# The second feed-forward's first rows, loaded ahead of the last two experts' scatters, and their transposes spread out

## The chip, the core and the metric

The kernel runs on one core of a Trainium2 chip. The metric is the device time of one execution in microseconds (us). Five engines work side by side, each through its own queue in order: TensorE (PE; its weight loads are listed as PEld), VectorE (DVE), ScalarE (ACT), GpSimd (POOL) and SyncE (SP), which issues most of the transfers (DMA). Semaphores order work between engines.

## What is computed

Three stages, each feeding the next, on 1536 tokens of 512 features in float32:

```python
# 1 attention, 2 x 8 heads, 768 positions, 64 wide: sinks 0..3 and a window of 128
a = softmax(where(keep, q @ k.T / 8, -1e9)); x = (a @ v)                     # -> 1536 x 512
# 2 mixture of experts: each token goes to one of 8 experts, at most 384 tokens each
e = argmax(x @ w_gate); h = relu(x[tokens of e] @ w1[e]); y = gate * (h @ w2[e])
# 3 second feed-forward, weights stored as 64-bit floats
out = square(relu(y @ w_in)) @ w_out                                         # 512 -> 2048 -> 512
```

Tokens that an expert has no place for give zeros.

## The kernel before, in words

Products are made three times over: each float32 factor is split into a high part (a copy rounded to the format fp32r, on ScalarE) and a low part (the difference, on VectorE), and high x high, high x low and low x high are summed in PSUM. So each weight and each activation costs ScalarE a copy and VectorE a subtraction (`split`, L141; `pre_split`, L704; L938 and L939; `go`, L1045 and L1046).

**Experts.** The tokens of an expert are worked in blocks of 128 rows. `body(e, b, ...)` (L905) is block b of expert e: the first product in two halves (`g1`), relu, transposes of the hidden values (`tr`, tiles hT, hTh, hTl), the second product in four groups of six matmuls (`g2`), the gate (L981, tile ys) and a scatter of the 128 rows by GpSimd into the table yd in DRAM (L982). Block (e, 0) always runs; `more` (L988) holds blocks 1 and 2 in branches that are taken when the expert has that many tokens (L994). In yd the rows are packed by expert, each with its token's number in an extra column; empty places go out of bounds and aren't written. `pre(e, b)` (L896) transposes a block's gathered rows into xT.

The order of the work is written out by hand. `body` has five points at which it runs functions handed to it (`also`), and a plan that says after which group how many `splits` run. For expert 7 the splits are ticks (`Ticks`, L191): each tick stages one piece of the second feed-forward's weights (1 MB: `piece_load`, L158; L180 to L188) through four steps on ScalarE and VectorE, and the plan LAST (L24) puts three ticks into block (7, 0). A piece's load goes out on SP as soon as the raw buffers that it needs are freed by an earlier split or tick (`freed`, `pull`).

**Second feed-forward.** It takes yd in three chunks of 512 rows. `load_y(c, tags)` (L1027) issues three loads of 128 rows each on SP (`ld`, L1034, tiles xb), and gives back four functions; function t (`go`, L1036) transposes tile t on TensorE (L1040, four transposes into one PSUM bank, tile x2T), copies the tokens' numbers on POOL (L1042), splits the result into the two x2A tiles (L1045, L1046) and, the first of them, issues the fourth load. For chunk 0, load_y is called when expert 7 begins, ahead of block (7, 0). Its loads depend on the scatters into yd that stand ahead of them in the program, so on those of experts 0 to 6. Where they have to be read again, since rows below 512 belong to expert 7, a branch behind expert 7 does so (L1097 to L1102): it compares `head`, the rows ahead of expert 7 (L1068), with 512. The functions 0 to 2 are run at point 4 of block (7, 0), behind its last `g2` and ahead of its last tick and of the gate; function 3 at point 0 of block (7, 1) (L1088, L1092).

Behind expert 7 come `ticks.close()` (L1108), twelve writes that clear the output (L1116), and the steps `stage_a` and `stage_b` (L1121, L1177), one tick beside each of the first.

By the reference's inputs the experts get 290, 123, 98, 163, 117, 165, 92 and 488 tokens, the last cut to 384. So there are 14 blocks, expert 5 has two, expert 6 one and expert 7 three, and 956 rows stand ahead of expert 6.

Of the kernel before, what the change touches and what calls it, by code (L numbers as in the profile page):

```python
# [16 lines left out]
P = 128  # L17
# [15 lines left out]
def kernel(  # L33
# [15 lines left out]
    nc = tc.nc  # L49
    B, H, S, D = q.shape  # L50
    NTOK, DM = out.shape
    E = w_gate.shape[1]
# [33 lines left out]
    def ps(tag, name):  # L86
        banks[tag].append(banks[tag].pop(0))
        return psum.tile([P, 512], F32, tag=f"b{banks[tag][-1]}", name=name)
# [127 lines left out]
    yd = dram.tile([NTOK, DM + 1], F32, name="yd")  # L216
# [107 lines left out]
    if fast:  # L324
# [22 lines left out]
        for g in range(3 if stack else 1):  # L347
            x = own[g * HS : (g + 1) * HS]
# [352 lines left out]
    def gate_at(e, b):  # L701
        return gate[2 + b % 2 if b else e % 2]
# [7 lines left out]
    def pre_gate(e, b, sums):  # L710
        g_ = gate_at(e, b)
        nc.vector.tensor_scalar(g_, sums, 1e-9, None, op0=ALU.add)
        nc.vector.reciprocal(g_, g_)
# [90 lines left out]
    for u in range(len(units) + PL + 1):  # L804
# [4 lines left out]
        if u < len(units):  # L809
            n, c = units[u]  # L810
# [17 lines left out]
        m, c = divmod(u, HP)  # L828
# [13 lines left out]
        if u % 4 == 2:  # L842
            r0 = u // 4 * P
# [41 lines left out]
    def x_at(e, b):  # L885
        return xring[min(b, XB - 1), e % 2]

    def load_x(e, b):
        if e >= E or b >= nblk:
            return  # L890
        nc.gpsimd.indirect_dma_start(
            out=x_at(e, b), out_offset=None, in_=xd[:, :], in_offset=bass.IndirectOffsetOnAxis(ap=src[:, b, e : e + 1], axis=0),
            bounds_check=NTOK - 1, oob_is_err=False,
        )

    def pre(e, b):  # L896
        if e >= E or b >= nblk:
            return
        p_ = ps("bg", "xT")
        for c in range(KD):  # L900
            nc.tensor.transpose(p_[:, c * P : (c + 1) * P], x_at(e, b)[:, c * P : (c + 1) * P], ident)
        pre_split(e, b, p_)
        pre_gate(e, b, x_at(e, b)[:, DM:])

    def body(e, b, splits, plan, also):  # L905
        xh, xl = xT[e, b]
        wts = W[e]
        splits = list(splits)

        def sp(n):  # L910
            for _ in range(n):
                if splits:
                    splits.pop(0)()

        hs = mp.tile([P, F], F32, tag="hs", name="hs", bufs=1)
        hp = [None, None]

        def g1(half, ks):
            if ks[0] == 0:
                hp[half] = ps("s" if half or b else "iv", "h")  # L920
            for kk in ks:
                r = slice(half * 512, half * 512 + 512)
                for m, (a, bb) in enumerate(((xh, wts.h), (xh, wts.l), (xl, wts.h))):
                    nc.tensor.matmul(hp[half], a[:, kk, :], bb[kk][:, r], start=(kk == 0 and m == 0), stop=(kk == KD - 1 and m == 2))

        def relu(half):
            nc.scalar.activation(hs[:, half * 512 : half * 512 + 512], hp[half], AF.Relu)

        hT = [None, None]

        def tr(half):
            p_ = ps("pt", "hT")
            for c in range(4):
                o0 = half * 512 + c * P
                nc.tensor.transpose(p_[:, c * P : (c + 1) * P], hs[:, o0 : o0 + P], ident)
            h_ = mp.tile([P, 512], F32R, tag="hTh", name="hTh", bufs=2)
            l_ = mp.tile([P, 512], F32R, tag="hTl", name="hTl", bufs=2)
            nc.scalar.copy(h_, p_)  # L938
            nc.vector.tensor_sub(l_, p_, h_.bitcast(F32))  # L939
            hT[half] = (h_, l_)  # L940

        y = ps("ot", "y")

        def g2(fs):
            for f in fs:
                h_, l_ = (x[:, (f % 4) * P : (f % 4 + 1) * P] for x in hT[f // 4])
                wh, wl = wts.h[KD + f // 2], wts.l[KD + f // 2]
                r = slice((f % 2) * 512, (f % 2) * 512 + 512)
                for m, (a, bb) in enumerate(((h_, wh), (h_, wl), (l_, wh))):
                    nc.tensor.matmul(y, a, bb[:, r], start=(f == 0 and m == 0), stop=(f == NF - 1 and m == 2))  # L950

        def point(i):
            for f in also.get(i, ()):
                f()

        plan = iter(plan)
        g1(0, [0, 1, 2, 3])
        sp(next(plan))
        relu(0)
        g1(1, [0, 1])  # L960
        sp(next(plan))
        tr(0)
        g1(1, [2, 3])
        sp(next(plan))
        relu(1)
        point(0)
        g2([0, 1])
        sp(next(plan))
        tr(1)
        point(1)  # L970
        g2([2, 3])
        point(2)
        sp(next(plan))
        g2([4, 5])
        point(3)
        g2([6, 7])
        point(4)
        sp(next(plan))
        y_ = mp.tile([P, DM + 1], F32, tag="ys", name="ys", bufs=2)
        nc.gpsimd.tensor_copy(y_.bitcast(I32)[:, DM:], src[:, b, e : e + 1])  # L980
        nc.vector.tensor_scalar(y_[:, :DM], y, gate_at(e, b), None, op0=ALU.mult)  # L981
        nc.gpsimd.indirect_dma_start(  # L982
            out=yd[:, :], out_offset=bass.IndirectOffsetOnAxis(ap=dst[:, b, e : e + 1], axis=0), in_=y_, in_offset=None,
            bounds_check=NTOK - 1, oob_is_err=False,
        )
        sp(len(splits))

    def more(e, b, also=()):  # L988
# [27 lines left out]
    def split_at(g, i):  # L1016
        W[g].split(i, nc.gpsimd if i in SPOOL else None, nc.vector.tensor_copy if i in SDVE else None)
# [6 lines left out]
    last = (E - 1) % 2  # L1024
    yts = [xring[b, 1 - last] for b in range(XB)]

    def load_y(c, tags):  # L1027

        c0, w = chunks[c]

        def ld(t):
            if t < w // P:
                r0 = c0 + t * P
                nc.sync.dma_start(yts[t % len(yts)], yd[r0 : r0 + P, :])  # L1034

        def go(t):  # L1036
            yt = yts[t % len(yts)]
            p_ = ps(tags[t % 2], "x2T")
            for kk in range(KD):
                nc.tensor.transpose(p_[:, kk * P : (kk + 1) * P], yt[:, kk * P : (kk + 1) * P], ident)  # L1040
            n = c0 // P + t
            nc.gpsimd.tensor_copy(tok[:, n : n + 1], yt.bitcast(I32)[:, DM:])  # L1042
            pv = p_.rearrange("p (k n) -> p k n", k=KD)
            hv, lv = (x[:, :, t * P : (t + 1) * P] for x in x2T[c])
            nc.scalar.copy(hv, pv)  # L1045
            nc.vector.tensor_sub(lv, pv, hv.bitcast(F32))  # L1046
            ld(t + len(yts))

        for t in range(len(yts)):
            ld(t)  # L1050
        return [lambda t=t: go(t) for t in range(w // P)]
# [8 lines left out]
    if nblk:  # L1060

        off = const.tile([P, E], F32, name="off")
        nc.vector.memset(off[:, 0:1], 0.0)  # L1063
        for e in range(1, E):
            nc.vector.tensor_add(off[:, e : e + 1], off[:, e - 1 : e], cntf[:, e - 1 : e])
        cnt = const.tile([P, E + 2], I32, name="cnt")
        nc.vector.tensor_copy(cnt[:, :E], cntf)
        nc.vector.tensor_copy(cnt[:, E : E + 1], off[:, E - 1 :])  # L1068
        nc.vector.tensor_add(cnt[:, E + 1 :], off[:, E - 1 :], cntf[:, E - 1 :])
        dst = const.tile([P, nblk, E], I32, name="dst")  # L1070
        nc.vector.tensor_add(free, free, spot.unsqueeze(2).to_broadcast([P, nblk, E]))
        nc.vector.tensor_add(dst, free, off.unsqueeze(1).to_broadcast([P, nblk, E]))
    vals = {}
    its = []
    for e in range(E):
        g = e + 1
        if e > 0:
            W[g].alloc()
        for b in range(1, XB):
            load_x(e + 1, b)  # L1080
        if g < E:
            splits = [(lambda i=i, g=g: split_at(g, i)) for i in range(16)]
        else:
            splits = [ticks.tick] * (NPRE + 1)
            its = load_y(0, ("bg", "bg"))
        if nblk:
            also = {2: [lambda: pre(e, 1), lambda: pre(e + 1, 0), lambda: load_x(e + 2, 0)]}
            also[4] = its[:-1]  # L1088
            body(e, 0, splits, HEAVY if g < E else LAST, also)
            if nblk > 1:  # L1090
                vals[e] = nc.values_load(cnt[0:1, e : e + 1], min_val=0, max_val=cap)
            more(e, 1, its[-1:])  # L1092
        else:
            for f in splits + its:
                f()
    if nblk:
        head = nc.values_load(cnt[0:1, E : E + 1], min_val=0, max_val=NTOK)  # L1097
        total = nc.values_load(cnt[0:1, E + 1 :], min_val=0, max_val=NTOK)

        with tc.If(head < CH):  # L1100
            for f in load_y(0, ("pt", "ot")):
                f()  # L1102
# [16 lines left out]
    outp, gT, its, scattered = {}, {}, [], []  # L1119
# [178 lines left out]
```

## Time and profile before

| | |
|---|---|
| median of 3 runs | 599.48 us (598.98 to 600.80) |
| the profiled execution | 599.34 us |
| its span, first to last instruction | 597.6 us |
| PE, PEld busy | 571.6 us (96%), 456.2 us (76%) |
| DVE, ACT, POOL busy | 354.2, 296.7, 138.8 us |
| bytes moved | 82.09 MB, mean 137 GB/s |

Times are from the span's start. Attention fills the first 130 us or so, the experts follow up to about 322 us, then the second feed-forward up to the end. "Busy" counts an engine's instructions that run, not how near they are to the engine's peak; the idle time of an engine that nobody waits for costs nothing.

### The profile page before, as it was taken

What the parts mean: (1) busy time and instruction counts of PE and PEld (TensorE: products, weight loads), DVE (VectorE), ACT (ScalarE), POOL (GpSimd) and SP (SyncE); (2) the same over time, 40 slices, a digit from 0 to 9 for tenths busy, and PEclk for the clock granted to TensorE, in tenths of its full rate; (3) what the DMA queues carried; (4) which work ended last, traced back from release to release, by engine and by line L of the source; (5) the groups of instructions that cost most, each with busy time, mean ns of one, the idle gap of its engine ahead of it and who ended that gap; (6) DMA issues with size and microseconds to landing.
All of it is one profiled execution on the core that took longest, in us unless ns stands there. A gap on an engine that the chain in (4) does not pass through costs nothing. (4 is left out here: it accounts for less than half of the span.)

```text
span 597.6 us, 9362 instructions
## 1 busy us (share of the span) xinstructions
PE 571.6 (96%) x3245; PEld 456.2 (76%) x3247; DVE 354.2 (59%) x838; ACT 296.7 (50%) x649; POOL 138.8 (23%) x235
## 2 busy tenths in 40 slices
PE   8999999989999999999899999999999999999994
PEld 4777777777887787777687677777888888888893
DVE  3788888758258857957853889886222232322222
ACT  4888888747247757737533455463222122222221
POOL 8544454244134413422111100000200000200002
PEclk9999999999999999999999999999999999999999
DMA  9688997457338975957731964521100000100001
GB/s 184 172 216 157 223 193 170 111 156 246 125 95 285 325 253 166 310 164 243 231 109 53 366 216 149 206 87 53 71 0 19 0 1 1 74 1 2 0 1 61
DMA packets 74625, 82.09 MB, mean 137 GB/s; under 512 B 42200, under 2 KB 53464, under 8 KB 74560
## 3 DMA queue, kind: packets, MB, share of 16 engines
q1 hardware_dynamic: 70608, 72.45, 41.8%
q0 software_dynamic: 3952, 8.82, 4.2%
q8 instruction: 35, 0.57, 0.4%
q14 instruction: 30, 0.25, 0.1%
HBM read 69.29 MB, written 16.08 MB: 143 GB/s over the span
## 5 line engine op out<-in xcount | busy, mean ns | idle before, releaser
L1140 DVE TENSOR_TENSOR xb<-xb 128x512 f32<-128x512 f32 (+1 forms) x48 | 31.6, 659 | 103.2 <-ACT xb L1139 103.2
L1139 ACT ACTIVATE xb<-a 128x512 f32<-128x512 f32 (+1 forms) x48 | 27.5, 573 | 111.8 <-PE a L1137 111.7
L454 ACT ACTIVATE p<-p,nm 128x260 f32<-128x260 f32 (+2 forms) x96 | 46.8, 489 | 17.3 <-DVE nm L442 16.0
L982 POOL DMA_INDIRECT yd<-ys,dst x14 | 26.3, 1881 | 114.3 <-DVE xl L145 32.5
L1163 POOL DMA_INDIRECT out_dram<-raw,tok x12 | 11.8, 986 | 168.8 <-issue 69.1
L1137 PE MATMUL a<-x2Ah,xh 128*128 128x512 f32 (+1 forms) x128 | 47.9, 374 | 0.3 <-PEq L1100 0.3
L1137 PE MATMUL a<-x2Ah,xl 128*128 128x512 f32 (+1 forms) x128 | 47.8, 374 | 0.0
L1137 PE MATMUL a<-x2Al,xh 128*128 128x512 f32 (+1 forms) x128 | 47.4, 374 | 0.0
L1196 PE MATMUL out<-yl,xT0h 128*128 128x512 f32 (+1 forms) x96 | 38.6, 402 | 4.9 <-DVE yl L188 4.9
L145 DVE TENSOR_TENSOR yl<-raw,yh 128x512 fp32r<-128x512 f32 x64 | 40.2, 686 | 4.6 <-ACT yh L144 4.1
L1196 PE MATMUL out<-yh,xT0h 128*128 128x512 f32 (+1 forms) x96 | 38.8, 405 | 0.4 <-ACT yh L186 0.4
L144 ACT CAST yh<-raw 128x512 fp32r<-128x512 f32 x64 | 35.3, 622 | 3.7 <-DVE off L1063 1.8
L1196 PE MATMUL out<-yh,gh 128*128 128x512 f32 (+1 forms) x92 | 36.4, 395 | 0.0
L1196 PE MATMUL out<-yl,gh 128*128 128x512 f32 (+1 forms) x92 | 36.3, 395 | 0.0
L144 ACT CAST xh<-raw 128x512 fp32r<-128x512 f32 x64 | 36.1, 619 | 0.3 <-ACTq L994 0.3
L939 DVE TENSOR_TENSOR hTl<-hT,hTh 128x512 fp32r<-128x512 f32 x28 | 19.3, 690 | 27.7 <-ACT hTh L938 27.7
L1196 PE MATMUL out<-yh,xT0l 128*128 128x512 f32 x88 | 34.8, 396 | 0.0
L1196 PE MATMUL out<-yh,gl 128*128 128x512 f32 x85 | 33.7, 396 | 0.0
L145 DVE TENSOR_TENSOR xl<-raw,xh 128x512 fp32r<-128x512 f32 x48 | 30.1, 686 | 1.9 <-ACT xh L144 1.8
L529 PE MATMUL ot<-pts,v 128*64 128x128 f32 x352 | 30.1, 286 | 0.5 <-ACT pts L496 0.5
L1155 ACT CAST xT0h<-xb 128x512 fp32r<-128x512 f32 (+1 forms) x24 | 14.3, 596 | 30.7 <-DVE xb L1140 30.7
L1155 ACT CAST gh<-xb 128x512 fp32r<-128x512 f32 (+1 forms) x23 | 13.7, 596 | 31.9 <-DVE xb L1140 31.9
(235 smaller groups left out, 1537.4 us busy)
## 6 DMA issues: line engine op xcount, KB each, us to landing
raw<-in_moe_w_dram SPq DMA_DIRECT2D x64, 512.0 KB, 5.7
raw<-in_moe_w_in_dram SPq DMA_DIRECT2D x16, 512.0 KB, 4.9
raw<-in_moe_w_out_dram SPq DMA_DIRECT2D x8, 1024.0 KB
yd<-zero SPq DMA_DIRECT2D x12, 256.5 KB, 5.4
xd<-x SPq DMA_DIRECT2D x12, 256.5 KB, 5.5
xb<-yd SPq DMA_DIRECT2D x12, 256.5 KB
kr<-in_k_dram SPq DMA_DIRECT2D x12, 256.0 KB, 4.7
qr<-in_q_dram SPq DMA_DIRECT2D x12, 256.0 KB, 7.3
```

Source lines behind the costliest of these rows:

```text
L144: (hi or nc.scalar.copy)(self.h[i][:, sl], t[:, sl])
L145: (eng or nc.vector).tensor_sub(self.l[i][:, sl], t[:, sl], self.h[i].bitcast(F32)[:, sl])
L454: nc.scalar.activation(d["p"][:, h, :width], d["p"][:, h, :width], AF.Exp, bias=d["nm"][:, h : h + 1], scale=-1.0, accum_out=d["sm"][:, h ...
L529: nc.tensor.matmul(d["o"][i * D : (i + 1) * D, c * P : (c + 1) * P], vt[b, kb][:, h, :], t_, start=i not in d["started"], stop=False, skip ...
L939: nc.vector.tensor_sub(l_, p_, h_.bitcast(F32))
L982: nc.gpsimd.indirect_dma_start(out=yd[:, :], out_offset=bass.IndirectOffsetOnAxis(ap=dst[:, b, e : e + 1], axis=0), in_=y_, in_offset=None ...
L1137: nc.tensor.matmul(a_[:, :w], a, bb, start=i == 0, stop=i == len(prods) - 1)
L1139: nc.scalar.activation(r_, a_[:, :w], AF.Relu)
L1140: nc.vector.tensor_mul(r_, r_, r_)
L1155: nc.scalar.copy(gh[:, :w], r_)
L1163: i = nc.gpsimd.indirect_dma_start(out=out, out_offset=bass.IndirectOffsetOnAxis(ap=tok[:rows, n : n + 1], axis=0), in_=o_[:rows, :], in_o ...
L1196: nc.tensor.matmul(o, a, bb[:, r], start=(f == 0 and m == 0), stop=(f == NFF - 1 and m == len(prods) - 1))
```

## The change

The loads of chunk 0 no longer depend on the scatters of expert 6: `body` collects its scatters by expert in `sent`, and `load_y` declares for each of its loads (the fourth too) that it doesn't depend on those of expert 6. `head` becomes the rows ahead of expert 6, so the branch that reads the rows again is taken when rows below 512 belong to expert 6 or 7. The functions 0, 1 and 2 move from point 4 of block (7, 0) to its points 1, 3 and 4: behind the second hT transposes, behind the third group of `g2`, and behind the fourth as before. Function 3 stays.

```diff
+    sent = {}
...
-        nc.gpsimd.indirect_dma_start(
+        i = nc.gpsimd.indirect_dma_start(
             out=yd[:, :], out_offset=bass.IndirectOffsetOnAxis(ap=dst[:, b, e : e + 1], axis=0), in_=y_, in_offset=None,
             bounds_check=NTOK - 1, oob_is_err=False,
         )
+        sent.setdefault(e, []).append(i)
...
-    def load_y(c, tags):
+    def load_y(c, tags, ahead=()):
...
-                nc.sync.dma_start(yts[t % len(yts)], yd[r0 : r0 + P, :])
+                i = nc.sync.dma_start(yts[t % len(yts)], yd[r0 : r0 + P, :])
+                for x in ahead:
+                    tc.declare_no_dep(i.ins, x.ins, reason="these rows are read again if one of them is that expert's")
...
-        nc.vector.tensor_copy(cnt[:, E : E + 1], off[:, E - 1 :])
+        nc.vector.tensor_copy(cnt[:, E : E + 1], off[:, E - 2 : E - 1])
...
-            its = load_y(0, ("bg", "bg"))
+
+            its = load_y(0, ("bg", "bg"), sent.get(E - 2, ()))
...
-            also[4] = its[:-1]
+            for i, f in zip((1, 3, 4), its):
+                also.setdefault(i, []).append(f)
```

## Rows read from the trace of the kernel before

**Rows 1.** Chain that ended last: start us, us, engine, tile, line.

```profile
323.34 1.24 DVE yl L188
...
338.49 7.13 DMA raw<-in_moe_w_out_dram
...
404.34 2.83 PE out L1196 x11
```

**Rows 2.** TensorE's waits, 255 to 410 us: total us, times, longest us.

```profile
PE x2T L1040 <- DMA xb<-yd: 1.9, 2, 1.6
```

**Rows 3.** Timeline of TensorE: start us, us, what, count [idle before <-releaser].

```profile
287.60 0.48 PE L950 MATMUL y<-yh,hTh 128*128 128x512 f32 x1
...
289.08 0.60 PE L901 MATMUL xT<-ident,xb 128*128 128x128 f32 x4
...
292.08 0.39 PE L950 MATMUL y<-yh,hTl 128*128 128x512 f32 x1
294.08 0.66 PE L1040 MATMUL x2T<-ident,xb 128*128 128x128 f32 x4 [1.61 <-DMA xb<-yd]
...
296.14 0.66 PE L1040 MATMUL x2T<-ident,xb 128*128 128x128 f32 x4 [0.53 <-DVE x2Al L1046]
296.67 0.49 PE L924 MATMUL h<-yh,xT1h 128*128 128x512 f32 x1
...
302.78 0.60 PE L1040 MATMUL x2T<-ident,xb 128*128 128x128 f32 x4
303.14 0.48 PE L950 MATMUL y<-yh,hTh 128*128 128x512 f32 x1
...
303.69 0.40 PE L950 MATMUL y<-yh,hTl 128*128 128x512 f32 x1
```

**Rows 4.** Timeline of VectorE, blocks (7,0) and (7,1).

```profile
289.07 0.68 DVE L939 TENSOR_TENSOR hTl<-hT,hTh 128x512 fp32r<-128x512 f32 x1
290.33 0.69 DVE L708 TENSOR_TENSOR xT1l<-xT,xT1h 128x512 fp32r<-128x512 f32 x1 [0.58 <-ACT xT1h L707]
...
296.27 0.69 DVE L1046 TENSOR_TENSOR x2Al<-x2T,x2Ah 128x512 fp32r<-128x512 f32 x1 [0.18 <-ACT x2Ah L1045]
297.45 0.69 DVE L1046 TENSOR_TENSOR x2Al<-x2T,x2Ah 128x512 fp32r<-128x512 f32 x1 [0.49 <-ACT x2Ah L1045]
...
302.85 0.68 DVE L939 TENSOR_TENSOR hTl<-hT,hTh 128x512 fp32r<-128x512 f32 x1
```

**Rows 5.** Timeline of SP's transfers, 283 to 292 us, all of them.

```profile
283.80 0.37 SPq L169 DMA_DIRECT2D raw<-in_moe_w_out_dram  x1
291.31 1.29 SPq L1034 DMA_DIRECT2D xb<-yd  x3
```

**Rows 6.** SP's waits, 250 to 345 us: total us, times, longest us.

```profile
SPq L1034 <- DMA yd<-ys,dst: 6.3, 1, 6.3
```

**Rows 7.** Line L1034, 280 to 300 us: its waiting instructions, ns min/median/max, first and last start.

```profile
L1034 SPq EVENT_SEMAPHORE  x5: 17/28/6243, 285.0 to 294.1; - x5
```

**Rows 8.** Timeline of POOL, the scatter of block (6,0).

```profile
282.15 2.54 POOL L982 DMA_INDIRECT yd<-ys,dst  x1 [10.21 <-issue]
```

**Rows 9.** Timeline of SP, the loads of chunk 1.

```profile
336.21 1.86 SPq L1034 DMA_DIRECT2D xb<-yd  x3
```

**Rows 10.** Timeline of POOL, first reader of chunk 1's loads.

```profile
340.93 2.55 POOL L1042 COPY tok<-xb 128x1 int32<-128x1 int32 x3 [15.51 <-DMA xb<-yd]
```

**Rows 11.** DMA queue, 287 to 288 us, then 289.5 to 291.3: packets, MB, share of 16 engines.

```profile
q1 hardware_dynamic: 86, 0.35, 95.8%
...
q1 hardware_dynamic: 12, 0.05, 6.1%
```

**Rows 12.** Stretches: us, busy of PE, PEld, DVE, ACT, POOL, granted clock, DMA share, GB/s.

```profile
292.50:294.00 1.50, 0.00 (x0) 0.00 (x0) 1.50 (x2) 0.00 (x0) 0.00 (x0) 1.00 0.85 290
592.00:594.00 2.00, 0.00 (x0) 0.00 (x0) 0.00 (x0) 0.00 (x0) 0.62 (x1) 1.00 0.64 244
595.00:597.00 2.00, 0.00 (x0) 0.00 (x0) 0.00 (x0) 0.00 (x0) 0.00 (x0) 0.50 0.00 0
```

## The prediction

> **What bounds the kernel now.** I read the chain of waits first. From 404.34 us on it is TensorE alone, and between 323.34 and 404 it is VectorE with one transfer, the load awaited for 7.13 us from 338.49 [rows 1]. The reader is to see where this stretch begins: with VectorE's L188 of the closing tick at 323.34, behind which SP's next piece load and the twelve clearing writes stand. So what makes expert 7's blocks end earlier or later moves everything behind it by as much. Second, TensorE's waits from 255 to 410 us: at the transposes of the second feed-forward's first rows (L1040) it waits 1.9 us in two times for their loads [rows 2]. Third, TensorE's timeline there: the last matmul of block (7,0) starts at 292.08 and is over at 292.3, and block (7,1) starts at 296.67 [rows 3]. That hole of 4.35 us is what the change aims at; three transposes of 0.36 us each lie in it (0.36 is 303.14 less 302.78, the price of the fourth, which runs with no wait).
>
> Fourth, and this decides, VectorE's timeline: between 289.07 and 302.85 it rests three times only, 0.58, 0.18 and 0.49 us, together 1.25 [rows 4]. At 302.85 it begins hTl of block (7,1), and TensorE takes that operand at 303.69, without a hole in its row of matmuls [rows 3]. VectorE is thus as full as TensorE in this stretch: TensorE's hole is covered by VectorE's arrears, the ticks' work on the pieces. At 303.69 the end is set by whichever of the two is later, and 0.84 us after the start of hTl is the earliest that TensorE can go on.
>
> **The change, part by part.** *The wait.* The three loads sit on SP behind the load of piece o0, issued at 283.80; they go out from 291.31 on [rows 5]. The first waits 6.3 us for a scatter into yd [rows 6]; the waiting begins just after 285.0 [rows 7]; the scatter is block (6,0)'s, on POOL from 282.15 to 284.7 [rows 8]. With that dependence gone the loads go out at about 285.05, 285.5 and 285.9. What stands ahead of them on SP is as before, o0's load among it.
>
> *The transposes.* They cost the same 3 x 0.36 us. The first now stands where TensorE arrives at 287.60 (behind the second hT transposes), the second behind two more groups of six matmuls and the xT transposes, the third behind one group more. Call t the moment when the first tile has landed and TensorE starts on it. Ahead of t nothing else of TensorE can run, since its queue is in order; and behind the first transposes are queued: six matmuls (1.48 us, 289.08 less 287.60), then the transposes of xT[7,1].
>
> *VectorE.* Its work is the same, in another order: the first subtraction (L1046) now stands ahead of xT1l and of the second tick, and waits. From transposes to subtraction it is 1.31 us (296.14 to 297.45); from the xT transposes to xT1l 1.25 us (289.08 to 290.33). So the first L1046 starts at t + 1.31. VectorE was free at 289.75 (289.07 and 0.68 of work), which is a rest of t - 288.44 where t is above that. The xT transposes start at t + 0.36 + 1.48 = t + 1.84, xT1l at t + 3.09; the subtraction was over at t + 1.99, a second rest of 1.10. All that follows finds its input ready: the second tile's subtraction stands behind the whole second tick. New rests: t - 287.34. Less the old 1.25, hTl of (7,1) moves by **t - 288.6**. For t at its earliest, 287.6, the first rest is none and the second 0.26 (VectorE free at 290.43, xT1l at 290.69), so the floor is -1.0.
>
> *TensorE's own path.* Block (7,1) would start at t + 6.1 and use hTl 7.0 us later, at t + 13.1; that is 305.1 for t = 292.0, under VectorE's 303.69 + 3.4 = 307.1. VectorE decides for every t considered; so even loads that come in time cannot give back the 2.9 us that TensorE's hole promises, only 1.0.
>
> *Where t lies.* The trace has no such load behind one piece of 1 MB alone, so bounds. In an idle queue the first tile took 294.08 - 291.31 = 2.77 us: t = 287.8. The same loads put behind other transfers at 336.21 [rows 9] reached their first reader at 340.93 [rows 10], 4.72 us: t = 289.8. The row that is nearest is o0's own transfer, which the loads would follow by 1.2 us. Its queue moves 0.35 MB in the microsecond from 287, the engines 95.8% busy; but from 289.5 to 291.3 twelve packets of it are still on their way at 6.1% of 16 engines, which is one engine that lags [rows 11]. Nothing else was issued on that queue between 283.80 and 291.31 [rows 5], so this is o0's tail. A tile is whole only when its share on that engine is, and with the loads queued behind, that share comes after about 291.2, with 0.8 us for it (256.5 KB at 0.35 MB/us is 0.73): t = 292.0. By the mean flow alone, without the tail, it is 289.5 + 0.73 = 290.2. I take 292.0, because the tail is of the very transfer in front, and keep 287.8 and 292.8 as ends. The sum: 292.0 - 288.6 = +3.4 us; by the mean flow +1.6.
>
> The Trainium skill's page "DMA: Bandwidth & Descriptors" (Queues, rings and completion order) says that each DMA engine takes the descriptors of one ring in order, and that a transfer's semaphore is complete only when every engine has landed its part. It speaks against this change and for +3.4 rather than +1.6; no row here shows single engines, only the 6.1%.
>
> *At nothing.* The fourth load now goes ahead of piece i2's on SP, and i2's, which follows the second tick's work on VectorE, goes about 3 us later than before; i2 is staged in the second feed-forward, behind 323.34 [rows 1], and if that cover were gone it would cost those 3 us. The row-number copies on POOL run earlier or later ahead of (7,0)'s scatter, whose rows are first read at 336. The PSUM bank that the second transposes need is free at t + 2.0, they come at t + 3.7. The branch compares rows ahead of expert 6 (956 by the reference's routing) with 512: not taken, as before.
>
> The profiled execution took 599.34 us, 0.14 under the median of 599.48; +3.4 gives 602.7 there and **602.9 us** on the median.
>
> **The rivals.** *In time (B).* The loads overtake or share with o0 and land by 287.6 to 288.4. For it: 2.77 us in an idle queue. Against it: 1 MB in front that needs 3 us. It gives -1.0 us, 598.5, and decides below t = 288.6; with t up to 290 it is +1.4 at most, still no measurable loss.
>
> *The wait stays (C).* If the loads still wait, by another scatter or the conditional blocks, for what ended at 291.31, the change doesn't do what it says, and the transposes stand too early: t = 294.08, +5.4 us, 604.9, and TensorE would stand for 6.5 us. For it: blocks of expert 6 and 7 lie in branches. Against: each of its scatters is named.
>
> *The clock falls (D).* TensorE would stand still from 287.6 to 292.0, 4.4 us. In the hole of before it stood 1.6 us and the clock stayed at 1.00; behind the kernel's last matmul (over at 590) it is 1.00 up to 594 and 0.50, the 1.2 GHz level, from 595 [rows 12]. At that level the 1.84 us between the first transposes and xT's become about 3.7 and, standing in VectorE's way, add 1.8: +5.2, 604.7; more if it lasts.
> The Trainium skill's page "TensorE: Matmul & The Clock Gate" (Why this matters for your kernels) warns of idle gaps between bursts of matmuls that drop the array to its half rate; whether 4.4 us is one, no row here shows.
>
> **How the numbers follow.** Forecast 0.60, B 0.22, C 0.08, D 0.10. Within 0.3% (1.8 us, about what a measurement of this kernel can tell from no change) lie nearly all of B and the part of the forecast with t under 290.4, some 0.09; faster by more would need gains that VectorE's arrears exclude, 0.04 for an error there. So slower 0.51 + 0.08 + 0.10 = 0.69, same 0.27, faster 0.04. The range: the forecast with both its ends of t that lie behind o0 (290.2 to 292.8: +1.6 to +4.2), C and most of D above, half of B below: 599.4 to 605.0. The likeliest case's own range is 601.1 to 603.7.
>
> **What would show it.** Right: the yd wait of L1034 is gone, its loads go out at 285; one wait of TensorE of some 4 us at the first L1040, none at the second and third; VectorE resting 2 to 4 us behind its hTl at 289; a new TensorE wait of about 2 us for hTl in block (7,1); block (7,0)'s remains and 323.34 shifted alike. Wrong: L1040 first at 287.6 to 288.5 (B), L1034 out at 291 (C), a granted clock under 1.00 near 292 (D), or a shift at 303.69 that the later stages don't keep.

## The result and the profile after

The changed kernel takes 603.98 us in the median of six runs, the kernel before 600.81 us in the six beside them: ratio 1.006, 95% interval 1.0041 to 1.0079, so 2.5 to 4.7 us slower. Forecast were 602.9 and slower by over 0.3%. The profiled execution of the changed kernel took 604.60 us (span 602.9), that of before 599.34 (span 597.6). The one of before is among the shorter of its kernel, that of the change among the longer, so their difference of 5.3 us is above the 3.2 of the medians; what goes with such differences between executions of one kernel is seen in the last section. Three executions far above the rest (630.83, 1058.9 and 1919.8 us) are left out of the comparisons below.

In the changed kernel the listing is shifted: `body`'s L924, L935, L939, L950, L981 are L926, L937, L941, L952, L983; `load_y`'s L1034, L1040, L1046 are L1037, L1045, L1051; L1196 is L1203.

TensorE's timeline of the changed kernel, the stretch of [rows 3]:

```profile
287.24 0.60 PE L937 MATMUL hT<-ident,hs 128*128 128x128 f32 x4
292.22 1.11 PE L1045 MATMUL x2T<-ident,xb 128*128 128x128 f32 x4 [4.39 <-DMA xb<-yd]
292.99 0.77 PE L952 MATMUL y<-yh,hTh 128*128 128x512 f32 x1
...
295.70 1.05 PE L901 MATMUL xT<-ident,xb 128*128 128x128 f32 x4
...
300.86 0.48 PE L926 MATMUL h<-yh,xT1h 128*128 128x512 f32 x1
...
307.18 0.60 PE L1045 MATMUL x2T<-ident,xb 128*128 128x128 f32 x4
308.63 0.48 PE L952 MATMUL y<-yh,hTh 128*128 128x512 f32 x1 [0.86 <-DVE ys L983]
```

The wait at the transposes has not gone, it has grown: one of 4.39 us at the first, where there were 1.61, 0.25 and 0.53 us at the three. It ends at 292.22. What follows runs slowly: from the first transposes to those of xT it is 3.48 us, where 1.84 were counted. And block (7,1) meets a new wait, for VectorE's ys.

SP's transfers from 282 to 300 us, and how long its instructions at L1037 waited from 284 to 286 us:

```profile
283.79 0.37 SPq L169 DMA_DIRECT2D raw<-in_moe_w_out_dram  x1
285.02 8.72 SPq L1037 DMA_DIRECT2D xb<-yd  x4
```

```profile
L1037 SPq EVENT_SEMAPHORE  x2: 17/17/17, 284.9 to 285.4; - x2
```

The dependence on expert 6's scatter is gone, as the change says: the loads go out from 285.02, at once, where the first waited up to 291.31 [rows 5]. They land only 2 us earlier for that.

VectorE's timeline of the changed kernel, the stretch of [rows 4]:

```profile
289.06 0.68 DVE L941 TENSOR_TENSOR hTl<-hT,hTh 128x512 fp32r<-128x512 f32 x1
293.99 0.69 DVE L1051 TENSOR_TENSOR x2Al<-x2T,x2Ah 128x512 fp32r<-128x512 f32 x1 [4.25 <-ACT x2Ah L1050]
297.41 0.69 DVE L708 TENSOR_TENSOR xT1l<-xT,xT1h 128x512 fp32r<-128x512 f32 x1 [2.72 <-ACT xT1h L707]
...
307.74 0.74 DVE L983 TENSOR_SCALAR ys<-y,gate 128x512 f32<-128x512 f32 x1
308.40 0.68 DVE L941 TENSOR_TENSOR hTl<-hT,hTh 128x512 fp32r<-128x512 f32 x1
```

Two rests, 4.25 and 2.72 us, where there were three of 1.25 together; after them VectorE works without a pause up to hTl of block (7,1), which begins 5.55 us later than in [rows 4].

The granted clock (the third number from the right) in stretches of the changed kernel:

```profile
289.00:291.00 2.00, 0.00 (x0) 0.00 (x0) 0.74 (x2) 0.00 (x0) 0.00 (x0) 1.00 1.01 389
291.00:293.00 2.00, 0.78 (x5) 0.78 (x5) 0.00 (x0) 0.00 (x0) 0.24 (x2) 0.57 0.24 90
293.00:295.00 2.00, 2.00 (x7) 1.61 (x6) 0.69 (x1) 0.59 (x1) 0.47 (x3) 0.50 0.28 80
...
297.00:299.00 2.00, 2.00 (x9) 1.62 (x8) 1.56 (x5) 2.00 (x3) 0.00 (x0) 0.72 0.00 0
299.00:301.00 2.00, 2.00 (x14) 1.69 (x13) 2.00 (x2) 0.98 (x2) 0.00 (x0) 1.00 0.00 0
```

TensorE had stood from 287.8 on; a little behind 291, still ahead of the first transposes, its clock fell to 0.50, the 1.2 GHz level, and it came back to 2.4 GHz in the stretch from 297.

The shift is kept behind expert 7. VectorE's closing tick (323.34 in [rows 1]) and TensorE's first matmul that waits for nothing later (404.34 there) are:

```profile
328.90 1.23 DVE L188 TENSOR_TENSOR yl<-raw,yh 128x1024 fp32r<-128x1024 f32 x1 [0.59 <-DVEq L1107]
```

```profile
409.62 0.50 PE L1203 MATMUL out<-yl,xT0h 128*128 128x512 f32 x1 [0.92 <-DVE yl L188]
```

They are 5.56 and 5.28 us later.

### The profile page after: what moved, and what is told of

Same layout as the page of the kernel before. It is cut to its first block, busy times and chain, and to the rows that moved or that the text cites. A ratio compares the mean times of both kernels' runs of the same rounds, so it can differ in the third digit from the quotient of the medians.

```text
span 602.9 us, 9364 instructions
## 1 busy us (share of the span) xinstructions
PE 572.8 (95%) x3247; PEld 457.4 (76%) x3247; DVE 354.3 (59%) x838; ACT 296.6 (49%) x649; POOL 138.4 (23%) x235
## 5 line engine op out<-in xcount | busy, mean ns | idle before, releaser
L1203 PE MATMUL out<-yl,xT0h 128*128 128x512 f32 (+1 forms) x96 | 38.6, 402 | 4.8 <-DVE yl L188 4.8
L1203 PE MATMUL out<-yh,xT0h 128*128 128x512 f32 (+1 forms) x96 | 38.7, 403 | 0.4 <-ACT yh L186 0.4
L1203 PE MATMUL out<-yh,gh 128*128 128x512 f32 (+1 forms) x92 | 36.4, 395 | 0.0
L1203 PE MATMUL out<-yl,gh 128*128 128x512 f32 (+1 forms) x92 | 36.4, 395 | 0.0
L941 DVE TENSOR_TENSOR hTl<-hT,hTh 128x512 fp32r<-128x512 f32 x28 | 19.3, 690 | 28.4 <-ACT hTh L940 28.4
L1203 PE MATMUL out<-yh,xT0l 128*128 128x512 f32 x88 | 34.8, 396 | 0.0
L1203 PE MATMUL out<-yh,gl 128*128 128x512 f32 x85 | 33.7, 396 | 0.0
L940 ACT CAST hTh<-hT 128x512 fp32r<-128x512 f32 x28 | 16.4, 587 | 26.4 <-PE hT L937 21.9
```

What stands on the lines that cost most here:

```text
L1203: nc.tensor.matmul(o, a, bb[:, r], start=(f == 0 and m == 0), stop=(f == NFF - 1 and m == len(prods) - 1))
```

## The experiments

Theory A is the forecast's: the loads land late since piece o0's 1 MB stands in front of them; the first transposes, now early in TensorE's queue, then hold up what is behind them; VectorE's arrears carry that on to block (7,1). The clock's fall is a second cost on top. Ten kernels took this apart; each was timed in five rounds beside the kernel before.

### Undoing one half: the transposes back at the end

```diff
-            for i, f in zip((1, 3, 4), its):
+            for i, f in zip((4, 4, 4), its):
```

> The change with the loads still ahead of expert 6's scatter, but all three transposes back at point 4 of block (7,0), where they were before. Theory A (the loads go out early but land at 292 behind piece o0, and what costs is what stands behind the first transposes in TensorE's and VectorE's queues): TensorE gets to the transposes at 292.3, when the first tile has just landed, VectorE is still busy with the second tick, and its two rests ahead of the later subtractions (0.18 and 0.49 us) go: 0.7 us under the kernel before, between 0.2 and 1.0, and the granted clock stays at 1.00. Rival R1 (the early loads themselves cost, by running beside o0 and the scatter): at least 2 us above the kernel before, wherever the transposes stand.

Measured: ratio 1.0001 (0.9985 to 1.0017). So the early loads by themselves cost nothing that shows, and R1, which asked for 2 us or more, falls. The 0.7 us of gain didn't come in the rows either: hTl of block (7,1) begins at 302.94, against 302.85. TensorE waits in another place, shown by its timeline and VectorE's:

```profile
292.57 1.38 PE L1045 MATMUL x2T<-ident,xb 128*128 128x128 f32 x8
296.23 0.66 PE L1045 MATMUL x2T<-ident,xb 128*128 128x128 f32 x4 [2.28 <-DVE x2Al L1051]
```

```profile
297.54 0.69 DVE L1051 TENSOR_TENSOR x2Al<-x2T,x2Ah 128x512 fp32r<-128x512 f32 x1 [0.77 <-ACT x2Ah L1050]
```

The tiles are there, but the third transposes need the PSUM bank of the first, and VectorE empties that only behind its second tick. One rest of 0.77 us stands where 0.18 and 0.49 were. This is the wait that the spreading would have removed.

### Undoing the other half: spread, but loaded as before

```diff
-            its = load_y(0, ("bg", "bg"), sent.get(E - 2, ()))
+            its = load_y(0, ("bg", "bg"))
```

> The transposes at points 1, 3 and 4 as in the change, but the loads wait for expert 6's scatter as before. Theory A: loads out at 291.3, first tile at 294.1, TensorE stands 6.5 us, hTl of block (7,1) moves by 294.1 - 288.6 = 5.5 us and by some 2 us more for the fallen clock: 7 to 8 us above the kernel before, ratio 1.011 to 1.014. Rival R1 (the early issue of the loads costs, not where the transposes stand): within 1 us of the kernel before.

Measured: ratio 1.0090 (1.0069 to 1.0112). With late loads the spreading is what costs, and R1 falls here too. It is less than expected: in the rows 0.9 us less, since in this execution the scatter landed earlier (loads out at 290.51, first transposes at 293.18), and 0.4 less for the clock.

```profile
293.18 1.11 PE L1045 MATMUL x2T<-ident,xb 128*128 128x128 f32 x4 [5.36 <-DMA xb<-yd]
```

```profile
309.02 0.68 DVE L941 TENSOR_TENSOR hTl<-hT,hTh 128x512 fp32r<-128x512 f32 x1
```

By t - 288.6 that is 4.6 us; hTl of block (7,1), at 309.02, is 6.2 us later than before, with the clock at 0.50 from 291 to 293 and still at 0.53 from 295 to 297.

### The clock taken out

```diff
             p_ = ps(tags[t % 2], "x2T")
+            for _ in range(18 if ahead and t == 0 else 0):
+                nc.tensor.matmul(p_, zb[:, :P], zb, start=True, stop=True)
```

> The change, with 18 matmuls on zeros (nobody reads their results) put ahead of the first transposes, so that TensorE works through most of its wait. Theory A with the clock as the second cost: first transposes at 292.2 as in the change, granted clock 1.00 throughout, VectorE's second rest falls from 2.72 to about 1.1 us, the gate's ys in block (7,0) and all behind it come 1.9 us earlier than in the change: 3.6 us above the kernel before, ratio 1.006. Rival R2 (the clock's fall is hidden and the late tile alone costs): the same time as the change.

Measured: ratio 1.0048 (1.0031 to 1.0064). TensorE's timeline, VectorE's, and the clock:

```profile
287.65 4.05 PE L1045 MATMUL x2T<-zb 128*128 128x512 bf16 x18
291.57 0.66 PE L1047 MATMUL x2T<-ident,xb 128*128 128x128 f32 x4
```

```profile
294.72 0.69 DVE L708 TENSOR_TENSOR xT1l<-xT,xT1h 128x512 fp32r<-128x512 f32 x1 [1.15 <-ACT xT1h L707]
...
305.72 0.68 DVE L941 TENSOR_TENSOR hTl<-hT,hTh 128x512 fp32r<-128x512 f32 x1
```

```profile
293.00:295.00 2.00, 2.00 (x12) 1.68 (x11) 0.85 (x2) 0.90 (x2) 0.26 (x2) 1.00 0.52 135
```

The clock stays at 1.00 through the wait and behind it, the second rest falls to 1.15 us, and hTl comes 2.87 us later than before: t - 288.6 gives 2.97 for t = 291.57. It is 2.68 us earlier than in the change, of which 0.65 is the earlier t and the other 2.0 the clock. R2 falls in the rows. In the medians the difference to the change is small (603.33 against 603.98 us), and the intervals overlap, so the times alone don't refute R2. In this execution something was lost later: the clock fell there too, behind holes of 0.68 and 0.92 us.

```profile
357.31 0.74 PE L1205 MATMUL out<-yl,xT0h 128*128 128x512 f32 x1 [0.92 <-DVE yl L188]
```

```profile
355.00:360.00 5.00, 3.40 (x9) 2.30 (x9) 4.97 (x6) 2.38 (x3) 0.00 (x0) 0.74 0.39 117
```

The matmul that began at 404.34 before begins at 408.02 here, so that the 2.9 us have become 3.7. The other eight executions, all with a mean clock of 0.996 or more, took 602.2 to 604.6 us, 2.9 to 5.2 above the 599.32 of the kernel before with such a clock; why most of them lost more than the 2.9 is open.

### Nothing in front

The load of o0 is held back until the three loads are issued (a list `shut`, filled at expert 6, stops the stream of loads at that piece):

```diff
-        while n and stream and held + stream[0][0] <= NRAW:
+        while n and stream and held + stream[0][0] <= NRAW and not (shut and len(stream) == len(order) - 2):
...
             its = load_y(0, ("bg", "bg"), sent.get(E - 2, ()))
+            shut.clear()
+            pull(NRAW)
```

> The change, with piece o0's load held back until the three loads have been issued, so that no 1 MB transfer stands in front of them. Theory A (the queue order sets the landing): first two loads out before 283, first tile there before TensorE arrives at 287.6, no wait at L1040, clock 1.00; VectorE's arrears then leave 1.0 us of gain over the kernel before (0.5 to 1.3), ratio 0.998. Rival R3 (the loads' landing hangs on the scatter of block (6,0), which lands at 291.2, or on their own latency, not on o0): first transposes at 291 or later, and the time of the change.

Measured: ratio 0.9969 (0.9955 to 0.9984), faster than the kernel before. SP, POOL's first reader, TensorE and VectorE:

```profile
282.19 2.27 SPq L1038 DMA_DIRECT2D xb<-yd  x3
284.55 0.39 SPq L170 DMA_DIRECT2D raw<-in_moe_w_out_dram  x1
```

```profile
287.25 1.04 POOL L1048 COPY tok<-xb 128x1 int32<-128x1 int32 x2 [2.33 <-DMA xb<-yd]
```

```profile
287.91 0.60 PE L1046 MATMUL x2T<-ident,xb 128*128 128x128 f32 x4
...
302.24 0.47 PE L953 MATMUL y<-yh,hTh 128*128 128x512 f32 x1 [0.86 <-DVE ys L984]
```

```profile
302.01 0.68 DVE L942 TENSOR_TENSOR hTl<-hT,hTh 128x512 fp32r<-128x512 f32 x1
```

The first tile is there at 287.25, TensorE takes it without a wait, and the end of VectorE's arrears sets block (7,1): hTl 0.84 us earlier than before (302.01 against 302.85), TensorE waiting 0.86 for ys just ahead of it. This execution was 0.23 us behind that of before already at hTl of block (7,0) (289.30 against 289.07), so like for like it is 1.07, and the floor of -1.0 holds in the rows (TensorE's stretch from 404.34 begins at 403.74). The measured times gain a little more, 0.9 to 2.7 us. Part of it may be the clock: nine of the eleven executions have a mean of 0.996 or more, and ten of the 25 beside them of the kernel before; among these the medians differ by 1.1 us (598.18 against 599.32). R3 falls: the scatter of block (6,0) is issued as before (282.38).

### Half in front

Piece o0's load is cut in two, the second half issued behind the loads:

```diff
+            for x in range(2):
+                def half(x=x):
+                    nc.sync.dma_start(
+                        t.rearrange("p (t n) -> p t n", t=2)[:, x : x + 1, :],
+                        w_out[2 * f * P : 2 * (f + 1) * P, :].rearrange("(t p) n -> p t n", p=P)[:, x : x + 1, :],
+                    )
+                if f == 0 and x:
+                    owed.append(half)
+                else:
+                    half()
...
             its = load_y(0, ("bg", "bg"), sent.get(E - 2, ()))
+            while owed:
+                owed.pop()()
```

> The change, with piece o0's load cut in two halves of 0.5 MB, the first ahead of the three loads and the second behind them. Theory A (each DMA queue works off what stands in front, so the landing goes with the size in front): the first transposes start between the 292.2 us of the change and the 287.9 us of the kernel with nothing in front, at 290 to 291; a wait of 2.4 to 3.4 us at L1045, hTl of block (7,1) later than before by 1.4 to 2.4 us (t - 288.6), the granted clock at 1.00 or falling for less long than in the change: ratio 1.002 to 1.005. Rival R4 (any transfer in front delays by its latency, whatever its size, or the scatter beside it does): 292 as in the change, ratio 1.006 or more.

Measured: ratio 1.0011 (0.9994 to 1.0028), its middle below what was expected; first transposes at 289.90. The executions fall into two groups. Five with a mean granted clock of 0.996 or more took 599.6 to 600.7 us, in the middle 0.8 above the executions of the kernel before with such a clock (599.38); of the six with less, five took 601.7 to 602.4 us, the profiled one (602.09) among them, 2.7 above. By t - 288.6 it should be 1.3 without the clock's fall. Where the clock fell in the executions that left no profile is not known.

With the same edit and nine matmuls on zeros ahead of the first transposes (the diff of "The clock taken out" with 9 for 18):

> Half of o0's load in front, with 9 matmuls on zeros ahead of the first transposes. Theory A (t - 288.6 and the clock's fall are two separate costs): first transposes at 289.9, granted clock 1.00, hTl of block (7,1) 1.3 us later than before, where the same kernel without the 9 matmuls had it 2.8 us later with the clock at 0.50 for some 3 us: profiled time 1.2 to 1.6 us under that kernel's 602.1. Rival R2 (the late tile alone costs): hTl 2.8 us later, as without them.

Measured: ratio 1.0038 (1.0023 to 1.0053). POOL's first reader, without and with the nine:

```profile
289.92 0.40 POOL L1055 COPY tok<-xb 128x1 int32<-128x1 int32 x2 [5.33 <-DMA xb<-yd]
```

```profile
289.72 0.18 POOL L1057 COPY tok<-xb 128x1 int32<-128x1 int32 x1 [5.11 <-DMA xb<-yd]
```

With all of o0 in front the first tile landed at 291.6 to 292.6 in four kernels, with half at 289.7 and 289.9, with nothing between 286.3 and 287.4 in four (the last three of them below). R4 falls, with one reserve: the half is freed and issued earlier, so the loads go out at 283.7, not 285.0, and 1.3 us of the earlier landing are only that; from issue to landing it is 6.6 to 7.6 us, 6.0 to 6.2, and 4.4 to 5.5.

In the rows the two costs come apart as expected. VectorE's hTl of block (7,1), with the nine matmuls and without:

```profile
303.85 0.68 DVE L949 TENSOR_TENSOR hTl<-hT,hTh 128x512 fp32r<-128x512 f32 x1
```

```profile
305.63 0.68 DVE L949 TENSOR_TENSOR hTl<-hT,hTh 128x512 fp32r<-128x512 f32 x1
```

It is 1.0 us later than before with them, and 2.8 without, where the clock reads:

```profile
290.00:291.00 1.00, 1.00 (x5) 0.91 (x6) 0.00 (x0) 0.18 (x1) 0.51 (x4) 0.60 0.56 227
291.00:292.00 1.00, 1.00 (x4) 0.80 (x3) 0.57 (x1) 0.40 (x1) 0.12 (x1) 0.50 0.14 47
```

The total didn't follow, and that part of the expectation failed: the execution with the nine took 604.24 us, and the median, 602.38, is above the 600.68 of the kernel without. Up to 404.34 the gain is kept (405.48 against 406.97 without); the timeline and clock far behind the experts show where that execution lost it:

```profile
519.78 0.35 PE L1156 MATMUL a<-x2Ah,xl 128*128 128x416 f32 x1 [2.06 <-issue]
```

```profile
520.00:525.00 5.00, 5.00 (x17) 3.91 (x16) 1.25 (x3) 1.05 (x2) 2.00 (x3) 0.66 0.43 161
```

Shortly behind the branch into the last chunk's code TensorE stood 2.06 us for nothing that the profile shows, and its clock fell behind it. No other execution read here has that hole. That it also raised the median is not shown, and the clock can't be all of it: the five executions with a mean of 0.996 or more still took 601.3 to 602.6 us. So this pair stands by its rows, not by its times.

### The first transposes behind xT's

```diff
-            for i, f in zip((1, 3, 4), its):
+            for i, f in zip((3, 4, 4), its):
```

> The change, with the first transposes at point 3 of block (7,0), behind the third group of matmuls, and the other two at point 4. Theory A (what costs is that the first transposes hold up the xT transposes and with them VectorE's second tick): the xT transposes run at 289.1 as before, TensorE waits 1.3 us at 290.9 for the tile, VectorE is busy with the second tick meanwhile; the third transposes wait for the bank of the first as in the kernels with all three at the end; the clock stays: within 0.3 us of the kernel before, ratio 1.000. Rival R7 (any wait of TensorE for the late tile is lost time, wherever it stands): 1.3 us above the kernel before or more.

The first transposes move from point 1 to point 3, the second from 3 to 4; those of xT, at point 2, are now ahead of both. Measured: ratio 0.9999 (0.9987 to 1.0011). TensorE's timeline:

```profile
289.03 0.60 PE L901 MATMUL xT<-ident,xb 128*128 128x128 f32 x4
291.59 0.66 PE L1045 MATMUL x2T<-ident,xb 128*128 128x128 f32 x4 [0.55 <-DMA xb<-yd]
...
296.03 0.81 PE L1045 MATMUL x2T<-ident,xb 128*128 128x128 f32 x4 [1.95 <-DVE x2Al L1051]
```

The loads are as late as in the change, but the xT transposes are ahead of them, VectorE has its second tick to work on, and the time is that of before. R7 falls. So the loss, but for the 0.7 us that the interval leaves, hangs on the first transposes standing ahead of xT's. The clock did not stay, as had been expected: in this execution it fell behind the hole of 1.95 us.

```profile
296.00:299.00 3.00, 2.97 (x10) 2.38 (x11) 2.08 (x4) 2.12 (x3) 0.00 (x0) 0.57 0.82 287
```

It took 600.38 us with a mean clock of 0.993; five others of this kernel, with 0.996 to 0.998, took 598.9 to 599.4, and the other six, with 0.992 and 0.993, 600.5 to 601.1.

### What the spreading is worth when the loads are in time

The kernel with nothing in front, with the transposes at point 4:

> The loads ahead of o0, but the three transposes back at point 4. Theory C (from the first run with the transposes at the end: the third needs the PSUM bank of the first, which VectorE frees only behind its second tick): TensorE waits some 2.3 us at the third transposes, VectorE rests 0.6 and 0.8 us, block (7,1) goes on as before: ratio 1.000 within 0.002, so the spreading is worth about 1 us once the loads are in time. Rival R6 (the loads in time are what helped, the places of the transposes nothing): 0.997 as with the transposes spread.

Measured: ratio 1.0012 (1.0000 to 1.0025). The third transposes wait for the bank:

```profile
296.08 0.65 PE L1046 MATMUL x2T<-ident,xb 128*128 128x128 f32 x4 [2.72 <-DVE x2Al L1052]
```

R6 falls. Spreading and loads in time gain together and neither alone.

### Less work for VectorE

The kernel with nothing in front, with the gate's product of block (7,0) on ScalarE ahead of the last tick:

```diff
         y_ = mp.tile([P, DM + 1], F32, tag="ys", name="ys", bufs=2)
+        lean = e == E - 1 and b == 0
+        if lean:
+            nc.scalar.activation(y_[:, :DM], y, AF.Copy, scale=gate_at(e, b))
+        sp(next(plan))
...
-        nc.vector.tensor_scalar(y_[:, :DM], y, gate_at(e, b), None, op0=ALU.mult)
+        if not lean:
+            nc.vector.tensor_scalar(y_[:, :DM], y, gate_at(e, b), None, op0=ALU.mult)
```

> The kernel with the loads ahead of o0, and the gate's product of block (7,0) (ys, 0.66 us of VectorE) moved to ScalarE ahead of the last tick. Theory B (VectorE's arrears set when block (7,1) goes on): TensorE's wait for ys (0.86 us) goes, hTl of block (7,1) starts 0.66 us earlier, at about 301.3, and the time is some 0.6 us under that of the kernel with the loads ahead of o0: ratio to the kernel before 0.996. Rival R5 (TensorE's own path or ScalarE's relu holds block (7,1), as its wait of 0.68 us for hs suggests): no change beside it, 0.997.

Measured: ratio 0.9967 (0.9955 to 0.9978), median 597.82 us. TensorE's first hole behind the fourth transposes is now for hTl alone:

```profile
301.79 0.50 PE L953 MATMUL y<-yh,hTl 128*128 128x512 f32 x1 [0.26 <-DVE hTl L942]
```

```profile
301.05 0.68 DVE L942 TENSOR_TENSOR hTl<-hT,hTh 128x512 fp32r<-128x512 f32 x1
```

hTl begins 0.96 us earlier than without the edit, and the stretch of 404.34 at 403.14, 0.6 earlier than without. Of both, 0.29 us are no gain: this execution was ahead by as much already at hTl of block (7,0) (289.01 against 289.30). That leaves 0.67 at hTl, as expected, and 0.3 at the later stretch. So theory B holds in the rows of block (7,1), against R5; the times of the two kernels can't be told apart. With the first tick begun earlier on top (its first part behind the first group of block (7,0)):

```diff
-LAST = (0, 0, 1, 0, 1, 1)
+LAST = (1, 0, 1, 0, 1, 1)
...
+        def begin(self):
+            piece_stage(self.seq[0], 0)
+            piece_stage(self.seq[0], 4)
+            self.begun = True
...
-            splits = [ticks.tick] * (NPRE + 1)
+            splits = [ticks.begin] + [ticks.tick] * (NPRE + 1)
```

> As the last, and the first tick begins earlier: its copy on ScalarE and two of its three VectorE steps stand behind the first group of block (7,0), in the 1.5 us in which VectorE rested ahead of 285.3. Theory B: another 1.2 to 1.5 us of arrears go, the waits of block (7,1) on ys, hs and hTl all but vanish and TensorE's own path takes over: 2.3 to 3.0 us under the kernel before in the profile, ratio 0.995 to 0.996. Rival R5: no faster than the kernel with the loads ahead of o0, 0.997, or slower by the 0.4 us that hTl of block (7,0) is delayed.

Measured: ratio 0.9974 (0.9964 to 0.9985), no gain. VectorE's timeline:

```profile
288.95 0.69 DVE L953 TENSOR_TENSOR hTl<-hT,hTh 128x512 fp32r<-128x512 f32 x1 [1.25 <-ACT hTh L952]
...
291.18 0.69 DVE L720 TENSOR_TENSOR xT1l<-xT,xT1h 128x512 fp32r<-128x512 f32 x1 [0.94 <-ACT xT1h L719]
```

The rest that was filled ahead of 285.3 comes back as rests of 1.25 and 0.94 us, in which VectorE waits for ScalarE's copies of what TensorE has just transposed. Its arrears begin only with the second tick, so work taken out ahead of 290 buys nothing: hTl of block (7,1) begins at 301.52, later than without. This expectation was wrong, and R5 is nearer. In this execution the clock fell besides, from 354 to 358 (0.50 from 355 to 357), behind holes of 1.11 and 0.93 us.

## Why the prediction was right, and where it was off

**Where t lies.** Predicted 292.0, found 292.22 in the profile, and 291.6 to 292.6 for the landing in the four kernels with all of o0 in front. Counting o0's lagging tail was right; the mean flow's 290.2 was not. While the loads follow, their queue is at work at full rate up to 291 and trails off behind it (DMA queue from 290 to 291, then from 291 to 292 us, as in [rows 11]):

```profile
q1 hardware_dynamic: 198, 0.38, 98.5%
...
q1 hardware_dynamic: 86, 0.15, 38.8%
```

That one engine lags is still read only from a share of 16 engines; which one, and why, was not tried, and that t came out this near may be in part luck. The Trainium skill's page "DMA: Bandwidth & Descriptors" (Queues, rings and completion order) says that an engine takes one ring's descriptors in order; the half and the empty front agree with it (landing 1.7 to 2.9 us and 4.2 to 6.3 us earlier than behind the whole, the half's issue being 1.3 us earlier).

**t - 288.6.** It held, within 0.2 us, wherever the clock did. The shift of hTl in block (7,1) against [rows 4], by kernel:

| kernel | t | t - 288.6 | hTl later by | granted clock behind t |
|---|---|---|---|---|
| o0 behind the loads | 287.91 | -0.7 (floor -1.0) | -0.84 | 1.00 |
| half in front, kept busy | 289.71 | 1.1 | 1.00 | 1.00 |
| half in front | 289.90 | 1.3 | 2.78 | falls to 0.50 |
| whole in front, kept busy | 291.57 | 3.0 | 2.87 | 1.00 |
| the change | 292.22 | 3.6 | 5.55 | at 0.50 from before t |
| spread alone | 293.18 | 4.6 | 6.17 | at 0.50 from before t |

So the step from the landing to the end, over VectorE's rests, was right, and with it that a landing in time gains 1.0 us and not 2.9.

**The clock (rival D).** Forecast with a chance of 0.10 and 1.8 us, and a clock under 1.00 near 292 was on the prediction's own list of signs against it; in the profile it came, and cost 1.9 us: 1.64 between the first transposes and xT's (3.48 against 1.84), the rest behind the start of the xT transposes, which take 1.05 us and not 0.60. The forecast and D were written as two cases, and in the profiled execution both are true together, 3.6 + 1.9. That is the step that was mis-sized: the stall and the fall it brings belonged in one sum. The measured difference, 2.5 to 4.7 us, holds the sum without the fall (3.6) and ends under the sum with it (5.5). That its middle, 3.2, is so near the forecast's 3.4 is in part luck: four of the six executions of before beside the change took 600.8 to 601.5 us, as executions of that kernel with a low mean clock do (last section), while the rows compare with one of 599.34. How often the clock fell in the executions that left no profile is open; all six of the change have a mean of 0.995 or less, eight of the nine with TensorE kept busy 0.996 or more. The Trainium skill's page "TensorE: Matmul & The Clock Gate" (Why this matters for your kernels) warns of such gaps; the trace agrees, with 4.39 us.

**The next wait.** Predicted was a wait of about 2 us for hTl in block (7,1). Found was one of 0.86 us for ys, a step ahead: the product y of block (7,1) needs the bank that ys empties. It is smaller than predicted since TensorE itself came 4.2 us later to that block (300.86 against 296.67), not 1.4. With TensorE kept busy it came 0.8 later (297.49); there it waits 0.85 us for ys and, ahead of it, 0.67 for ScalarE's hs, which the prediction didn't have.

**The rivals.** In time (B): not in the change; made so, it gives ratio 0.9969. The wait stays (C): no, L1037 doesn't wait. The parts counted at nothing (the fourth load, i2's, the row numbers, the branch) show no wait of TensorE or VectorE in the rows of after, though i2's load went out 7.1 us later (300.13 against 293.05), not 3.

## What to carry to other kernels

A load that is freed of a wait still stands behind what its queue was given before: look at what was issued in the microseconds ahead of it, and put the small load that is needed soon ahead of the large one that is needed late. An instruction that may wait belongs behind what others are waiting for on its engine: the same late tile cost nothing that could be told behind the xT transposes, and 2.5 to 4.7 us ahead of them. And where two engines are both full, a hole in one is worth only what the other can follow: here 1.0 of 2.9 us.

## What was not expected of the hardware

The clock can fall after holes much shorter than the 4.39 us of the change. In the kernel with half of o0 in front TensorE waited 2.17 us, up to 289.90, and the clock fell behind that, when matmuls were already running again. In three other kernels the holes near 295 were much alike, and the clock went its own way: it stayed at 1.00 through those of 2.28 and 2.72 us with all transposes at the end (loads behind o0 and ahead of it), and fell behind the one of 1.95 us with the first at point 3. In two executions it fell near 355 behind two holes of 0.7 to 1.1 us each. So the length of the hole alone doesn't say it. The mean granted clock of the timed executions runs from 0.990 to 0.998 for the kernel before, too. Of the 78 of it timed beside the experiments, 43 have 0.996 or more, and all but one of these took 599.0 to 600.2 us; of the 35 below, all but three took 600.1 to 603.6. The medians of the two groups are 1.3 us apart, so a difference of 0.2% between two kernels can be that, and not their work.
